# Cutting the last two query groups into units of two head slots by 128 queries, with one more joint maximum unit

## The chip, the cores and the metric

The kernel runs on one core of a Trainium2 chip. A core has TensorE (PE, matrix products), VectorE (DVE), ScalarE (ACT), GpSimd (POOL) and a queue engine (SP) that issues the transfers. Each works through its own list of instructions in order and waits for the others by semaphores. The metric is device microseconds of one execution, lower is better. The kernel before takes 1231.28 us, the median of 3 runs (1231.07 to 1231.67).

## The reference

One transformer block on 2048 tokens of width 512, batch 1, in bf16: LayerNorm, attention with 32 heads of 16 channels, output projection and residual, LayerNorm again, and a gated feed-forward layer of width 1792 with a second residual.

```python
    def _A_ref(x, wqkv, wo):
        ...
        qkv = (lambda x, *d: x.transpose(*d))((x @ wqkv).reshape(B, S, 3, H, Dh), 2, 0, 3, 1, 4)
        q, k, v = qkv[0], qkv[1], qkv[2]
        scores = jnp.einsum("bhqd,bhkd->bhqk", q, k) * (Dh ** -0.5)
        p = _softmax(scores, axis=-1)
        o = jnp.einsum("bhqk,bhkd->bhqd", p, v)
        return (lambda x, *d: x.transpose(*d))(o, 0, 2, 1, 3).reshape(B, S, D) @ wo

    def _B_ref(x, w_gate, w_up, w_down):
        return (_gelu(x @ w_gate) * (x @ w_up)) @ w_down

    x = A_x
    h = x + _A_ref(_layernorm(x, axis=-1), A_wqkv, A_wo)
    h2 = h + _B_ref(_layernorm(h, axis=-1), B_w_gate, B_w_up, B_w_down)
    return h2
```

## The kernel before

The 2048 tokens are cut into 8 groups (gi, 0 to 7) of 256 queries, and the 32 heads into 8 slots of 4 heads. A slot's 4 heads lie on the four row groups of 32 partitions, so four heads' products can stand side by side in PE's array. One unit (ui) is one group and one slot, 64 units in all, numbered group by group. A unit has 16 ticks, and the loop over ticks writes the instructions of all engines out in their order. That order is fixed when the program is built: a stream of dense work (projections, feed-forward) is fitted in by a planner (`Dense`, `PoolStream`) that keeps estimates of how far ACT and POOL have fallen behind.

Each unit is passed twice. The first pass (`p1_pair`, L841; `p1_consume`, L856) makes scores with the queries on the partitions, 512 keys at a time, and DVE reduces them to row maxima, one instruction over 1024 columns a tick. POOL turns the maxima into three bf16 pieces (`negm_pre`), a transposing transfer brings them to the key side, and POOL adds them to the spare rows of Q (L905), so that the second pass gets scores with the maximum already taken off. The second pass (`p2_tile`, L921; `p2_consume`, L950) runs 24 ticks later (16 + LAGX): scores with the keys on the partitions, 128 keys by 256 queries a matmul, two matmuls to a bank of 512 columns, and one Exp of 512 columns on ACT for each bank. Two such tiles belong to a tick. `item_pv` (L964) multiplies the exps with V, four heads side by side, in four steps a unit of 16 matmuls each. A 17th column of ones in V gives the sums. `o_turn` and `o_norm` (L998, L1002) transpose the result by a transfer and divide on POOL into `Otok`.

A unit in JOINT is a joint maximum unit. PE makes the differences of two key blocks for two heads, ACT takes their Relu into RB, and DVE adds and maximises in one pass (L853): two instructions over 512 columns take the place of two over 1024, and the unit loses one tick.

When a group's 8 slots are done, its 2 x 128 tokens get output projection and residual (`item_oproj`), LayerNorm on POOL, a transposing transfer into `hnT_l`, and then the feed-forward layer in the loop of the next groups: seven pairs `item_gate`, `item_up` (L1198, 256 columns), evacuated by ACT (L685), gelu by POOL's polynomial and a Tanh on ACT (L1178, L1186 to L1190), product on POOL (L1242), and two `item_down` (L1250). Where a tick has no dense work, filler matmuls keep PE going (`dummy`, L1410).

The end is different, since nothing is left to hide the last group behind. After tick 1024 no maxima are left; the 24 ticks of exps still due follow as exps of 1024 columns (`p2_pair`, L938), two to a block, with the dense items between the blocks. The flag `dve_free` then sends evacuations to DVE. The POOL and PE orders stay fixed: an instruction that waits holds everything behind it on its engine. Then `tail_b` does the rest for all 256 tokens of group 7: norm of the last slot (`tail_norm`), transposes, projection (L1361), bn_stats and scaling on DVE (L1364 to L1375) with a power on POOL (L1373), transposes (`tail_hnT`, L1335), and gate, up and down straight on PE, with Gelu on ACT (L1211) and the product on DVE (L1227).

## Time and profile before

| what | us |
|---|---|
| median of 3 runs | 1231.28 |
| the profiled execution | 1231.23 |
| its span, first to last instruction | 1229.3 |
| busy in the span: PE, DVE, ACT, POOL | 1104.8, 1175.8, 1189.5, 834.6 |
| end of the last maximum (DVE) | 1176.85 |
| end of the last exp (ACT) | 1200.10 |
| first gate matmul of the end | 1207.85 |
| end of the last copy before the store (ACT) | 1226.92 |

All places in the profile are counted from the start of the span; the execution's own time is 1.9 us longer than the span. The granted clock of TensorE is 1.0 throughout. Rows of groups read: line, engine, operation, tiles and shapes, count, then busy time, mean ns of one, and idle time of that engine ahead of them. Rows of stages read: stretch, length, then busy us and count of PE, PE's weight loads, DVE, ACT and POOL, granted clock, share of the DMA engines and GB/s. Rows of the order in time read: start, length of the merged row, engine, line, operation, tiles and shapes, count. A PE row's length includes the way through the array, so neighbours overlap; the pace is read from the starts. The chain's rows are start, length, engine, tile and line.

### The profile page before, as it was taken

Reading aid. Unit: us, or ns where it says so; the run is one execution under the profiler, and the core shown is the slowest. Engines: PE = TensorE matmul, PEld = TensorE weight load, DVE = VectorE, ACT = ScalarE, POOL = GpSimd, SP = SyncE. Lnnn points to the kernel's source line nnn. Section 1 sums busy time; section 2 is a strip of 40 time slices with the busy share of each in tenths; the row PEclk is TensorE's granted clock in tenths of the full one; section 3 lists DMA queues with packets and bytes.
Section 4 is the critical chain, followed back from the end, with each engine's and each line's share of the span. In section 5 each row is a group of like instructions: output and inputs, shape, how many; then the busy total and the mean of one; then the engine's idle time right before and its main releaser. Section 6 shows DMA issues by size and latency. Waiting matters only on the chain.

```text
span 1229.3 us, 31435 instructions
## 1 busy us (share of the span) xinstructions
PE 1104.8 (90%) x12462; PEld 429.5 (35%) x12598; DVE 1175.8 (96%) x1111; ACT 1189.5 (97%) x2417; POOL 834.6 (68%) x1760
## 2 busy tenths in 40 slices
PE   7899988889998989898989989999888988889898
PEld 3233232233333333333332333333333333333335
DVE  8999999999999999999999999999999999999933
ACT  7899999999999999999999999999999999999993
POOL 7567684766776586757768477775867777548850
PEclk9999999999999999999999999999999999999999
DMA  4111114200010000100011000100001100010000
GB/s 153 27 34 27 29 26 136 87 10 9 8 27 21 14 9 8 31 21 7 11 25 18 17 11 7 28 21 13 10 8 26 27 8 11 18 32 10 8 19 14
DMA packets 68658, 31.54 MB, mean 26 GB/s; under 512 B 53920, under 2 KB 67488, under 8 KB 68512
## 3 DMA queue, kind: packets, MB, share of 16 engines
q1 hardware_dynamic: 68512, 29.52, 9.5%
q8 instruction: 101, 1.65, 0.5%
q14 instruction: 45, 0.37, 0.1%
HBM read 11.80 MB, written 2.10 MB: 11 GB/s over the span
## 4 chain that ended last, share of the span: by engine, by line
ACT 57%; DVE 29%; PE 8%; issue 3%; POOL 2%; DMA 0%; POOLq 0%; DVEq 0%
ACT PTM L950 32%; DVE PM L856 29%; ACT PTG L950 10%; ACT PTE L950 6%; PE pbank L1250 2%; ACT g_sb L685 2%; ACT u_sb L685 2%; ACT th_sb L1178 2%; PE pbank L841 1%; PE pbank L921 1%; PE pbank L1198 1%; ACT OB L685 1%; PE pbank L443 1%; DVE OA L853 1%; PE pbank L1410 1%
## 5 line engine op out<-in xcount | busy, mean ns | idle before, releaser
L856 DVE TENSOR_REDUCE PM<-pbank 128x2 f32<-128x1024 f32 x998 | 1135.9, 1212 | 8.3 <-PE pbank L921 3.8
L950 ACT ACTIVATE PTM<-pbank 128x512 bf16<-128x512 f32 x1357 | 731.9, 719 | 3.9 <-PE pbank L921 0.4
L921 PE MATMUL pbank<-QT,KT 32*128 32x256 bf16 x4096 | 503.0, 273 | 14.8 <-ACT PTM L950 7.6
L841 PE MATMUL pbank<-KT,QT 32*128 32x512 bf16 x2022 | 388.6, 384 | 31.5 <-DVE PM L856 11.8
L1410 PE MATMUL pbank<-ones_bf,ident 128*128 128x512 bf16 x708 | 221.4, 384 | 52.2 <-ACT PTM L950 22.5
L950 ACT ACTIVATE PTG<-pbank 128x512 bf16<-128x512 f32 x407 | 224.8, 704 | 1.7 <-PE pbank L921 1.3
L841 PEld LDWEIGHTS pbank<-KT,QT 32*128 32x128 bf16 x2022 | 97.9, 90 | 363.4 <-DVE PM L856 139.0
L921 PEld LDWEIGHTS pbank<-QT,KT 32*128 32x128 bf16 x4096 | 170.3, 92 | 75.9 <-ACT PTM L950 40.4
L950 ACT ACTIVATE PTE<-pbank 128x512 bf16<-128x512 f32 x236 | 139.3, 717 | 1.3 <-PE pbank L921 0.9
L964 PE MATMUL pbank<-PTM,VA 128*17 128x256 bf16 x2776 | 125.4, 274 | 1.5
L998 POOL TENSOR_TENSOR LINV<-OBT,negone 128x8 f32<-128x8 bf16 x62 | 103.5, 1670 | 2.7 <-DMA OBT<-OB 2.7
L1188 POOL TENSOR_TENSOR th_sb<-g_sb 128x512 f32<-128x512 f32 x49 | 51.0, 1041 | 76.5 <-ACT g_sb L685 76.5
L1410 PEld LDWEIGHTS pbank<-ones_bf,ident 128*128 128x128 bf16 x810 | 47.8, 97 | 149.1 <-ACT PTM L950 94.9
L964 PEld LDWEIGHTS pbank<-PTM,VA 128*17 128x17 bf16 x2776 | 60.0, 89 | 45.5 <-issue 29.8
L1198 PE MATMUL pbank<-hnT_l,wg_sb 128*128 128x256 bf16 x448 | 67.0, 275 | 4.1 <-ACT PTM L950 0.9
L1198 PE MATMUL pbank<-hnT_l,wu_sb 128*128 128x256 bf16 x448 | 67.1, 275 | 2.1
L1187 POOL TENSOR_TENSOR th_sb<-th_sb,g_sb 128x512 f32<-128x512 f32 x49 | 62.3, 1270 | 4.1
L1190 POOL TENSOR_TENSOR th_sb<-th_sb,g_sb 128x512 f32<-128x512 f32 x49 | 62.1, 1268 | 1.7
L1242 POOL TENSOR_TENSOR GUT<-th_sb,u_sb 128x512 bf16<-128x512 f32 x49 | 62.1, 1268 | 1.2
L1250 PE MATMUL pbank<-wd_sb,GUT 128*128 128x512 bf16 x209 | 57.7, 382 | 2.8 <-ACT PTM L950 1.3
L905 POOL TENSOR_TENSOR QT<-QT,STG 128x256 bf16<-128x256 bf16 x64 | 42.8, 669 | 23.0 <-DMA STG<-ST 22.3
L1186 POOL TENSOR_SCALAR th_sb<-th_sb 128x512 f32<-128x512 f32 x49 | 30.4, 620 | 39.7 <-ACT th_sb L1178 39.7
(168 smaller groups left out, 1130.2 us busy)
## 6 DMA issues: line engine op xcount, KB each, us to landing
QKS<-QKS SPq DMA_DIRECT2D x27, 112.0 KB, 2.1
x_sb<-in_A_x_dram SPq DMA_DIRECT2D x4, 512.0 KB, 5.7
xres<-in_A_x_dram SPq DMA_DIRECT2D x16, 128.0 KB, 2.3
out_dram<-out_sb SPq DMA_DIRECT2D x16, 128.0 KB, 1.7
wg_sb<-in_B_w_gate_dram SPq DMA_DIRECT2D x4, 448.0 KB, 4.3
wu_sb<-in_B_w_up_dram SPq DMA_DIRECT2D x4, 448.0 KB, 3.9
wd_sb<-in_B_w_down_dram SPq DMA_DIRECT2D x3, 512.0 KB, 4.3
STG<-ST SPq DMA_TRANSPOSE x64, 2.3
```

Of the source, the lines that this page charges most:

```text
L841: P.op("pe", lambda e, g=g, b=b: e.matmul(pbank[:, b, :], QT[32 * g:32 * g + 32, c, slot, 128 * qt:128 * qt + 128], KT[32 * g:32 * g + 32, ...
L856: P.op("dve", lambda e: e.tensor_reduce(out=PM[:, par, qt, kc, g:g + 2], in_=pbank[:, b:b + 2, :], axis=AX.X, op=ALU.max), reads=[("pb", b ...
L921: P.op("pe", lambda e, kt=kt, i=i: e.matmul(pbank[:, b, 256 * i:256 * i + 256], KT[32 * g:32 * g + 32, slot, 128 * kt:128 * kt + 128], QT[ ...
L950: P.op("act", lambda e, b=b, pi=pi: e.activation(out=PTt(pi), in_=pbank[:, b, :], func=ACT.Exp), reads=[("pb", b)], writes=[("PT", pi)], e ...
L964: P.op("pe", lambda e, g=g, kt=kt, pi=pi, i=i: e.matmul(pbank[32 * g:32 * g + 17, b, 0:256], VA[:, kt, 4 * slot + g, :], PTt(pi)[:, 256 * ...
L998: P.op("pool", lambda e: e.tensor_tensor(out=li, in0=o4[:, :, :, 16], in1=negone[:, 0:8].rearrange("p (q h) -> p q h", q=2), op=ALU.pow), ...
L1187: o(1.27, lambda e: e.tensor_tensor(out=ts_, in0=ts_, in1=gs, op=ALU.mult), [("th", par), ("g", par)])], then=done)
L1190: o(1.27, lambda e: e.tensor_tensor(out=ts_, in0=ts_, in1=gs, op=ALU.mult), [("th", par), ("g", par)])], then=poly_done)
L1198: P.op("pe", lambda e, dc=dc, fc=fc, i=i: e.matmul(pbank[:, b, 256 * i:256 * i + 256], w[:, dc, 128 * fc:128 * fc + 128], hT[:, dc, :], st ...
L1242: P.op("pool", lambda e: e.tensor_tensor(out=o_ap, in0=shp(ts_), in1=shp(us), op=ALU.mult), reads=[("th", par), ("u", par)], writes=o_keys ...
L1250: P.op("pe", lambda e: e.matmul(pbank[:, b, :], GUT[:, fc, 128 * k:128 * k + 128], wd_sb[:, fc, :], start=first, stop=last), reads=[("GUT" ...
L1410: P.op("pe", lambda e: e.matmul(pbank[:, b, :], ident[:], ones_bf[:, 0:512], start=True, stop=True), reads=["ident", "ones_bf"], writes=[( ...
```

## The change

Groups 6 and 7 (GH = 6 and up) keep 8 units each, but a unit there is two slots by 128 queries: first the four slot pairs with the group's first 128 queries (half 0), then the same four with the second 128 (half 1). So a group's first 128 tokens have all heads after four units. A second-pass bank holds four matmuls of 128 columns, and a V step has 32 matmuls of 128 columns.

Group 6's feed-forward is done per half, in items of four chunks of 128 channels (`item_gate_h`, `item_up_h`, the last of two chunks). Group 7's first half goes through projection, LayerNorm and transposes behind tick 1024 (`item_oprojA`, `item_hnA`), with DVE and one POOL power, and its gate and up products are written out raw to GA and UA (`item_raw`) between the last exps; `tail_b` takes their gelu and product, and their down projection, beside the second half's norm. Only the second half then has gate, up and down at the very end (`tail_gate`, `tail_up`, `end_mm`), the down product as two halves of 256 columns with two stores. `item_down` may start behind tick 1024 without the planner's other conditions, and raw items are sorted ahead of it. The last unit's V steps come in two items. Unit 60, the first of group 7's second half, becomes the 14th joint unit. The diff, cut to its core:

```diff
+PV_TL = (9, 10, 17, 18)
+DOWN_AT = 2
+A_LATE = True
+GH = 6
-JOINT = (5, 9, 12, 14, 17, 20, 25, 28, 33, 36, 41, 44, 49)
+JOINT = (5, 9, 12, 14, 17, 20, 25, 28, 33, 36, 41, 44, 49, 60)
...
+        GA = at("GA", [128, NFC, 128], FP32, 0)
+        UA = at("UA", [128, NFC, 128], FP32, NSLOT * 512 * 2)
...
-        units = [(gi, slot) for gi in range(NG) for slot in range(NSLOT)]
+        UB = GH * NSLOT
+        units = [(gi, slot) for gi in range(GH) for slot in range(NSLOT)] + [(gi, 2 * sp) for gi in range(GH, NG) for _ in range(2) for sp in range(NSLOT // 2)]
+        half = lambda ui: (ui - UB) // (NSLOT // 2) % 2
+        def part(ui, qh):
+            gi, slot = units[ui]
+            hf = gi % 2
+            return (slot, 2 * hf + qh) if ui < UB else (slot + qh, 2 * hf + half(ui))
...
-            if it[0] is item_down and it[1] == (GL - 1, 1) and not force[0]:
+            if it[0] is item_down and not force[0] and not dve_free[0] and (tight() or dense.now // 16 in JOINT and dense.now % 16 > J_GONE - 6 or act_lag[0] > LAG_START):
                 return False
...
+            n, q0, kt0 = 2, 256 * hf, 2 * m
+            if ui >= UB:
+                slot, qt = part(ui, m // 4)
+                n, q0, kt0 = 4, 128 * qt, 4 * (m % 4)
+            qn = 512 // n
+            for i in range(n):
+                kt = kt0 + i
+                P.op("pe", lambda e, kt=kt, i=i: e.matmul(pbank[:, b, qn * i:qn * i + qn], KT[32 * g:32 * g + 32, slot, 128 * kt:128 * kt + 128],
+                                                          QT[32 * g:32 * g + 32, c, slot, q0:q0 + qn], start=True, stop=True, tile_position=(32 * g, 0)),
...
+        def add_ffn_half(gi, k):
+            for t in range(NTL):
+                dense.add(item_gate_h, gi, k, t, est=3)
+                dense.add(item_up_h, gi, k, t, est=3)
...
+        def item_oprojA(b):
...
+            P.op("dve", lambda e: e.bn_stats(out=stats2[:, t, :], in_=pbank[:, b, :]), reads=[("pb", b)], writes=[("stats2", t)])
+            P.op("dve", lambda e: e.tensor_copy(out=hh, in_=pbank[:, b, :]), reads=[("pb", b)], writes=[("h", GL % 2, 0)])
+            P.op("dve", lambda e: e.bn_aggr(out=mv2[:, t, :], in_=stats2[:, t, :]), reads=[("stats2", t)], writes=[("mv2", t)])
...
+            def rest():
+                P.op("dve", lambda e: e.tensor_scalar(out=hn_sb[:, 0, :], in0=hh, scalar1=mv2[:, t, 0:1], scalar2=rstd2[:, tt], op0=ALU.subtract, op1=ALU.mult),
...
+                dense.add(item_hnA, front=True, est=1, not_before=dense.now + 1)
+            pool.add([(0.6, lambda: P.op("pool", lambda e: e.tensor_tensor(out=rstd2[:, tt], in0=rstd2[:, tt], in1=nhalf[:, 0:1], op=ALU.pow), reads=[("rstd2", t), "nhalf"], writes=[("rstd2", t)]))], then=lambda: defer(1, rest), front=True)
...
+        def half_mms(b, gi, k, t, w, nm, hr):
+            fcs = chunks(t)
+            for i, fc in enumerate(fcs):
+                for dc in range(4):
+                    P.op("pe", lambda e, dc=dc, fc=fc, i=i: e.matmul(pbank[:, b, 128 * i:128 * i + 128], w[:, dc, 128 * fc:128 * fc + 128], hnT_l[gi % 2][:, dc, 128 * k:128 * k + 128], start=(dc == 0), stop=(dc == 3)),
...
+        def item_raw(b, t, w, nm, dst, key):
+            yield from half_mms(b, GL, 0, t, w, nm, [("hnT", GL % 2, 0)])
...
+            evac_act(dst[:, 4 * t:4 * t + n, :].rearrange("p c s -> p (c s)"), pbank[:, b, 0:128 * n], [("pb", b)], [(key, t)], extra=dQ)
...
+            for t in range(NTL):
+                raw_gelu(t)
+            raw_mult(0)
...
+            end_h()
+            gb = [4, 5, 6, 7, 3]
+            for t in range(NTL):
+                tail_gate(gb[2 * t % 5], t)
+                tail_up(gb[(2 * t + 1) % 5], t)
+                if t == 0:
+                    for fc in range(8, NFC):
+                        down_mm(0, GL, 0, fc)
...
+                if t >= 2:
+                    for q in range(2):
+                        end_mm(q, chunks(t - 2))
+            for q in range(2):
+                end_mm(q, range(4 * (NTL - 2), NFC))
```

478 lines of the change are left out of this document (297 added, 181 removed).

## The prediction

> **What bounds the kernel now.** I read the page first, then the list of groups for the stretch that the change touches, then busy time by stage, then the chain that ended last, and last the order of time on each engine behind the attention loop.
>
> ```profile
> span 1229.3 us, 31435 instructions
> PE 1104.8 (90%) x12462; PEld 429.5 (35%) x12598; DVE 1175.8 (96%) x1111; ACT 1189.5 (97%) x2417; POOL 834.6 (68%) x1760
> ```
> ```profile
> L856 DVE TENSOR_REDUCE PM<-pbank 128x2 f32<-128x1024 f32 x237 | 269.5, 1212 | 1.6 <-PE pbank L921 1.1
> L921 PE MATMUL pbank<-QT,KT 32*128 32x256 bf16 x952 | 117.6, 273 | 3.3 <-ACT PTM L950 1.9 <-ACT PTG L950 0.5
> L1410 PE MATMUL pbank<-ones_bf,ident 128*128 128x512 bf16 x150 | 47.2, 384 | 16.0 <-ACT PTM L950 9.0 <-ACT PTG L950 1.3 <-ACT OB L685 1.3
> ```
> ```profile
> 905.00:1176.85 271.85, 242.10 (x2860) 95.50 (x2888) 270.24 (x241) 269.62 (x557) 194.28 (x399) 1.00 0.07 17
> 1176.85:1200.12 23.27, 22.02 (x268) 9.39 (x272) 1.97 (x4) 22.98 (x29) 10.55 (x16) 1.00 0.07 21
> 1200.12:1207.85 7.73, 7.46 (x56) 3.50 (x49) 4.25 (x13) 3.65 (x6) 0.70 (x1) 1.00 0.00 0
> 1207.85:1229.30 21.45, 18.32 (x138) 13.60 (x140) 5.53 (x8) 4.78 (x8) 0.00 (x0) 1.00 0.06 20
> ```
> ```profile
> 1140.01 0.49 ACT u_sb L685
> ...
> 1154.08 22.76 DVE PM L856 x20
> ...
> 1223.69 2.60 PE pbank L1250 x12
> 1226.32 0.60 ACT out_sb L1403
> ```
>
> The shares of the page hide four stages with three different limits. In the attention loop (to 1176.85) DVE is the bound: 237 maxima stand idle 1.6 us together, and twenty of them take 22.76 us, 1.138 us each: one tick. ACT is nearly full beside it. From 1176.85 to 1200.12 the exps of the last 24 ticks drain on ACT (22.98 of 23.27 us busy; DVE 1.97). From there to 1207.85 runs a chain of small steps (last head's norm, output projection, LayerNorm), and from 1207.85 PE alone is the bound: gate, up and down of the last 256 tokens, 18.4 us of matmuls end to end, then one copy and the store.
>
> In the programs' order both kernels are alike until the add of unit 48's maximum (L905), near 905 us, so nothing can move ahead of that.
>
> **The change part by part.** Everything below is set against this profiled execution: span 1229.3, its own time 1231.23, which is 0.05 under the median of the three runs shown (1231.28).
>
> *Units of two slots by 128 queries (groups 6 and 7).* A score tile is four matmuls of 128 moving columns where it was two of 256; each step of probabilities times V is 32 where it was 16. Same columns, twice the weight loads. What a 128-column matmul costs with a weight load of its own:
>
> ```profile
> 10.15 1.06 PE L421 MATMUL pbank<-ident,xn_sb 128*128 128x128 bf16 x16
> ```
> ```profile
> L1335 PE MATMUL pbank<-ident,OnT 128*128 128x128 bf16 x8 | 0.7, 222 | 0.1
> ```
> ```profile
> 1167.53 0.39 PE L921 MATMUL pbank<-QT,KT 32*128 32x256 bf16 x2 [0.44 <-ACT PTM L950]
> 1168.40 0.39 PE L841 MATMUL pbank<-KT,QT 32*128 32x512 bf16 x2
> 1168.40 0.50 PE L921 MATMUL pbank<-QT,KT 32*128 32x256 bf16 x4
> 1168.83 0.40 PE L964 MATMUL pbank<-PTG,VA 128*17 128x256 bf16 x8
> 1169.05 0.39 PE L964 MATMUL pbank<-PTM,VA 128*17 128x256 bf16 x8
> 1169.38 0.39 PE L841 MATMUL pbank<-KT,QT 32*128 32x512 bf16 x2
> ```
>
> Sixteen transposes in 1.06 us, less the 0.22 that one takes, are 56 ns apart. Two score matmuls of one row group take 0.39 with 0.27 for the second: 120 ns apart for 256 columns. So a tile streams for 120+107 = 227 ns now and about 67+55+55+53 = 230 ns afterwards. V: 16 from 1168.83 to 1169.44 (four side by side, 109 ns a round) become 8 rounds of 56, 448 for 436 ns. A tick with a whole V step takes PE 0.98 us (1168.40 to 1169.38) against DVE's 1.138, and the 150 filler matmuls (L1410) of the stretch give way too. Cost 0; were the cover gone, 64 V steps by 12 ns plus 28 half FFN items by 24 ns would be 1.4 us. The FFN of group 6 is done in two halves of 128 tokens: the same columns again, the first half four units earlier, and ACT's evacuations and tanhs add up to the same in 512-column pieces. Group 6's first down projection moves from the end into the loop, where PE has room.
>
> *The 14th joint unit.* One maximum over 1024 columns falls out and another becomes two of 512:
>
> ```profile
> 915.04 0.68 DVE L853 CUSTOM_DVE_ANT_0 OA<-pbank,OA 128x512 f32<-128x512 f32 x1
> 915.65 0.69 DVE L853 CUSTOM_DVE_ANT_0 OA<-pbank,OA 128x512 f32<-128x512 f32 x1
> 916.26 9.29 DVE L856 TENSOR_REDUCE PM<-pbank 128x2 f32<-128x1024 f32 x8
> ```
>
> 915.04 to 916.26 is 1.22, in place of 2 x 1.138: DVE gains 1.06 us. ACT pays two Relus (0.49 each, as its other 512-column evacuations) and catches up two exps. If ACT can't, nothing is gained (bound 0). I take -0.8, near the full gain, because the moved FFN half leaves the last units of the loop less gelu work.
>
> *The drain.* It now holds the output projection and LayerNorm of the last group's first 128 tokens, and their gate and up (8 items, 112 matmuls by 56 ns), evacuated by the idle DVE.
>
> ```profile
> 1177.36 2.85 ACT L938 ACTIVATE PTG<-pbank 128x1024 bf16<-128x1024 f32 x3 [0.27 <-PE pbank L921]
> 1182.80 0.67 ACT L1178 ACTIVATE th_sb<-th_sb 128x512 f32<-128x512 f32 x1
> 1196.11 3.99 ACT L938 ACTIVATE PTM<-pbank 128x1024 bf16<-128x1024 f32 x4
> 1180.06 1.67 POOL L998 TENSOR_TENSOR LINV<-OBT,negone 128x8 f32<-128x8 bf16 x1
> 1205.40 0.70 POOL L1373 TENSOR_TENSOR rstd<-rstd,nhalf 128x2 f32<-128x2 f32 x1 [12.15 <-DVE rstd L1372]
> ```
>
> 24 exps of 1024 columns by 0.926 and one tanh (0.52 of path) make the 22.74 us from 1177.36 to 1200.10. The tanh is of 256 columns now (-0.2). PE is in order, and the transposes of the normalised half (item_hnA) stand behind the third block of scores. Counted from the last maximum: projection done 1.6; bn_stats 0.7, copy 0.65, aggregate and add 0.4: 3.35; the power and its two hops 0.88; scaling 0.4, transposes 0.4, copy 0.4: 5.5; first raw gate 0.9; then the fourth block of scores at 6.5, with its first exp at 6.9, where ACT is free at 6.06. **Stall 0.85.** On POOL the power (0.70) now stands ahead of a reciprocal (1.67) and the last unit's add, which ends at 6.5: the last unit is the fifth block, so that is in time. After that a block has 1.85 us and PE needs 1.7 to 2.0 (24 x 56 ns, or 64 V matmuls, scores 0.23, three changes of array form at some 0.11), so ACT stays the bound, narrowly. Sum +0.65; bounds -0.2 (no stall) and +3 (PE late by 0.3 in each of ten blocks).
>
> *From the last exp to the last gate input.* Before 7.75 us.
>
> ```profile
> 1195.56 0.69 DVE L674 CAST out_sb<-pbank 128x512 bf16<-128x512 f32 x1 [4.52 <-PE pbank L1255]
> 1200.60 0.42 DVE L674 COPY OA<-pbank 128x256 f32<-128x256 f32 x1 [4.35 <-PE pbank L964]
> 1203.61 0.70 DVE L1364 BATCH_NORM_STATS2 stats<-pbank 128x6 f32<-128x512 f32 x1 [0.57 <-PE pbank L1361]
> 1206.21 0.73 DVE L1375 TENSOR_SCALAR OnT<-xres,mv,rstd 128x512 bf16<-128x512 bf16 x2 [0.88 <-POOL rstd L1373]
> ```
>
> One token tile instead of two saves a bn_stats (0.6), half of each copy and one projection matmul (0.7 together). But eleven down matmuls and the residual (12 x 0.215 = 2.6) now stand on PE right ahead of the last V step, and the cast of 0.69 ahead of the OA copy on DVE: the V step ends some 0.9 later against the last exp. And four down matmuls and two residual ones (1.1) stand between the transposes and the first gate, of which 0.2 is covered. I get 7.5: -0.25, bounds -1.4 and +1. The four gelus of the raw half (0.6 each) and the table load lie beside this chain on ACT.
>
> *Gate, up and down at the end.*
>
> ```profile
> 1207.85 1.03 PE L1198 MATMUL pbank<-hnT_l,wg_sb 128*128 128x256 bf16 x8
> 1208.72 1.04 PE L1198 MATMUL pbank<-hnT_l,wu_sb 128*128 128x256 bf16 x8
> 1223.53 2.75 PE L1250 MATMUL pbank<-wd_sb,GUT 128*128 128x512 bf16 x12
> ```
> ```profile
> L1250 PE MATMUL pbank<-wd_sb,GUT 128*128 128x512 bf16 x53 | 13.1, 379 | 0.2
> L1410 PE MATMUL pbank<-ones_bf,ident 128*128 128x512 bf16 x31 | 8.4, 381 | 0.6 <-issue 0.3 <-DVE OA L674 0.3
> L1227 DVE TENSOR_TENSOR GUT<-pbank,th_sb 128x512 bf16<-128x512 f32 x7 | 4.8, 692 | 11.8 <-PE pbank L1198 11.8
> L1211 ACT ACTIVATE th_sb<-pbank 128x512 f32<-128x512 f32 x7 | 4.2, 597 | 11.6 <-PE pbank L1198 11.6
> ```
>
> Now: 112 matmuls of 256 at 109 ns (8 in 0.87) and 28 of 512 at 0.215 (12 in 2.75, of which the last takes 0.38), 18.44 us from 1207.85 to the last one's end. Afterwards: 112 of 128 at 56 ns = 6.27, six left-over down matmuls 1.29, 28 of 256 at 109 = 3.05, and 0.2 of latency: 10.8. ACT's gelu (0.6) and DVE's product (0.69) stay under PE's 0.9 an item. -7.64.
>
> By the Trainium skill, "TensorE: Matmul & The Clock Gate", section Back-to-back issue gap, a stream of load and matmul pairs sustains one per about 81 ns at 128 columns. By that the sum would be 112 x 25 ns = 2.8 us higher; the sixteen transposes at 56 ns speak against it here.
>
> *Store.* The last copy is 256 wide, 0.4 for 0.60 us; two half stores in place of one: -0.2.
>
> **Sum:** -0.8 + 0 + 0.65 - 0.25 - 7.64 - 0.2 = -8.24. 1231.23 - 8.24 = **1223.0 us**.
>
> **The rivals.**
>
> *PE becomes the bound in the last two groups (slower).* If a matmul can't start faster than its weight load allows, width no longer counts: at the 120 ns that the score matmuls show now, a tile would take 0.48 for 0.23 and a V step 0.87 for 0.44. Per tick, with a V step in one of four, +0.25+0.11 = 0.36 us, less PE's slack of 1.138-0.98 = 0.16: +0.2 in 240 ticks, 48 us, time about 1271. It decides from the point where the excess eats 8.24 us, 0.034 a tick: six extra spacings a tick, so (0.16+0.034)/6 = 32 ns each, 88 ns a matmul. For it: loads of one row group follow one another, and no row shows four 128-wide matmuls in one row group. Against it: the transposes, and L1198 with 109 ns a matmul, which is all stream.
> The Trainium skill has the rule behind it (same page, section The mechanism of packing small matmuls): a weight load overlaps running matmuls only where the row group differs. By that rule each load would stand open, as in this rival. The 109 ns of L1198, all rows of the array, don't agree with it.
>
> *The drain goes to PE.* Stalls of 0.3 us in every block, or the LayerNorm chain late by more than a block: +3 in place of +0.65, near 1225.5. For it: PE has 22.02 of 23.27 us busy there already. Against it: 31 matmuls behind 1177 are filler (L1410, 8.4 us), most of them in the drain.
>
> *The joint unit doesn't fit.* ACT, at 269.62 of 271.85, takes the two Relus on the path: +1 in place of -0.8, near 1224.8.
>
> *No change.* The end chain's new order costs what the halved FFN saves: it needs 7.6 us more between the last exp and the last gate, where every step is shown at 0.2 to 0.9. 1231.
>
> **How the numbers follow.** Forecast 0.61, drain on PE 0.16, joint unit 0.09, PE-bound groups 0.11, no change 0.03. A change of under 0.2% (2.5 us) can't be told from none. Faster: 0.61+0.16+0.09 = 0.86; same 0.03; slower 0.11. The lower end takes the favourable bounds (joint -1.06, drain -0.2, chain -1.4: 1220.8) and some room, 1219.5; the upper end takes the drain and the joint unit together (1227.2) with room, 1228.5. Left out: slower 0.11, same 0.03, and 0.04 at the ends.
>
> **What would show it.** The last maximum should end 0.5 to 1 us earlier; score matmuls of 128 should start some 56 to 67 ns apart in a row group, and DVE's idle time before maxima stay near 2 us behind 905. In the drain one idle gap of ACT near 0.9 us before the fourth block; from the last exp to the first tail gate about 7.5 us; from there to the last matmul 10.8. Wrong would be: maxima that wait for PE throughout groups 6 and 7, a drain over 26 us, or tail gates 80 ns or more apart.

## The result and the profile after

The changed kernel takes 1225.16 us (median of 4 runs, 1224.78 to 1225.74) beside 1231.43 (4 runs, 1231.07 to 1231.67) for the kernel before: a ratio of 0.995, 95% interval 0.9932 to 0.9967. The forecast was 1223.0 with a range of 1219.5 to 1228.5. The profiled execution, the longest of the four, took 1225.74 us, 5.5 less than that of before; 8.2 were forecast. By the median 2.2 us are missing against the forecast, in the profiles 2.7; what follows says where these 2.7 us are.

The page of the changed kernel first (span; busy time of each engine), then its busy time by stage (stretch, length, busy us and count of PE, PE's weight loads, DVE, ACT and POOL, granted clock, DMA share, GB/s), cut at the last maximum, the last exp and the first tail gate:

```profile
span 1224.0 us, 36091 instructions
PE 1130.3 (92%) x14845; PEld 476.7 (39%) x14845; DVE 1181.1 (96%) x1124; ACT 1190.3 (97%) x2421; POOL 841.3 (69%) x1774
```
```profile
905.00:1177.75 272.75, 255.29 (x4825) 140.94 (x4823) 270.35 (x243) 271.16 (x561) 194.75 (x403) 1.00 0.09 18
1177.75:1201.76 24.01, 22.54 (x535) 15.88 (x536) 9.27 (x21) 23.13 (x28) 14.08 (x23) 1.00 0.08 19
1201.76:1210.51 8.75, 6.27 (x94) 3.12 (x91) 4.82 (x11) 4.33 (x8) 4.17 (x4) 1.00 0.05 17
1210.51:1224.00 13.49, 10.77 (x148) 9.49 (x145) 2.92 (x5) 3.16 (x6) 0.00 (x0) 1.00 0.07 21
```

The stages stand one under the other, and against before's they read so:

| stage | before | after | forecast of the difference | measured |
|---|---|---|---|---|
| loop, to the last maximum | 1176.84 | 1177.75 | -0.8 | +0.91 |
| drain, to the last exp | 23.26 | 24.01 | +0.65 | +0.75 |
| last exp to first tail gate | 7.75 | 8.75 | -0.25 | +1.00 |
| gate, up, down to the last matmul | 18.43 | 10.77 | -7.64 | -7.66 |
| last copy and store | 3.00 | 2.69 | -0.2 | -0.31 |

The last column adds up to the spans' own difference, -5.31 us; another 0.18 of the 5.5 lies outside the spans. So the large term was right to 0.02 us, the drain to 0.1, and two small ones had the wrong sign: the loop is 1.7 us longer than forecast and the chain behind the last exp 1.25 us.

The widths first. These rows are the order in time on PE, in the loop and at the first tail gates:

```profile
1168.52 0.39 PE L943 MATMUL pbank<-QT,KT 32*128 32x128 bf16 x4
...
1210.51 1.06 PE L1292 MATMUL pbank<-hnT_l,wg_sb 128*128 128x128 bf16 x16
1211.40 1.06 PE L1292 MATMUL pbank<-hnT_l,wu_sb 128*128 128x128 bf16 x16
```

Four score matmuls of 128 columns in one row group take 0.39 us with 0.22 for the last, so they start 57 ns apart; sixteen gate matmuls take 0.89 from 1210.51 to 1211.40, 56 ns each. A load does not hold a narrow matmul up, in one row group or over the whole array. The rival with PE as the bound is gone, and so is the 81 ns of the Trainium skill ("TensorE: Matmul & The Clock Gate", section Back-to-back issue gap): no run here shows it.

The drain, on ACT (the bracket is ACT's idle time ahead of the row and what ended it):

```profile
1182.22 1.94 ACT L960 ACTIVATE PTM<-pbank 128x1024 bf16<-128x1024 f32 x2 [0.40 <-PE pbank L943]
1184.65 3.85 ACT L960 ACTIVATE PTM<-pbank 128x1024 bf16<-128x1024 f32 x4 [0.48 <-PE pbank L943]
```

The forecast had one stall of 0.85 us before the fourth block. There are two, 0.40 before the third and 0.48 before the fourth, 0.88 together, and nothing behind them: PE keeps up, if narrowly (22.54 of 24.01 us busy).

The chain behind the last exp, which ends at 1201.76. On PE, DVE and POOL in order of time:

```profile
1199.48 2.55 PE L1391 MATMUL pbank<-wd_sb,GUT 128*128 128x512 bf16 x11
1202.63 0.62 PE L989 MATMUL pbank<-PTM,VA 128*17 128x128 bf16 x32
...
1206.66 0.68 DVE L1490 TENSOR_TENSOR GUT<-GA,UA 128x512 bf16<-128x512 f32 x1
1206.82 0.93 POOL L1543 TENSOR_TENSOR rstd<-rstd,nhalf 128x1 f32<-128x1 f32 x1 [1.68 <-DVE rstd L1542]
1207.73 1.26 POOL L1490 TENSOR_TENSOR GUT<-GA,UA 128x512 bf16<-128x512 f32 x1
1207.87 1.27 DVE L1547 TENSOR_SCALAR OnT<-xres,mv,rstd 128x512 bf16<-128x512 bf16 x1 [0.52 <-POOL rstd L1543]
...
1209.19 0.40 PE L1469 MATMUL pbank<-ident,OnT 128*128 128x128 bf16 x4 [2.08 <-DVE OnT L1547]
```

The last V step ends at 1203.25, 1.49 us behind the last exp (some 0.5 before), held up by eleven down matmuls; the forecast had 0.9 of that delay. What was not: the scaling on DVE takes 1.27 us (the forecast took 0.4 from the same operation) while a POOL product of 1.26 us (1207.73) runs beside it, with a second one behind that; and the power takes 0.93 us where the row of before has 0.70, beside a DVE product. (Before had two columns there; the same power on one column took 0.58 us in the drain, L1207.) Against the rows of before that is 1.1 us on the chain.

In the loop, DVE's idle time before maxima is 2.4 us from 905 on (1.6 before), so within the forecast's "near 2", and still the last maximum is late:

```profile
L867 DVE TENSOR_REDUCE PM<-pbank 128x2 f32<-128x1024 f32 x235 | 268.5, 1214 | 2.4 <-PE pbank L943 1.3
```

### The profile page after: what moved, and what is told of

Same layout as the page of the kernel before. It is cut to its first block, busy times and chain, and to the rows that moved or that the text cites. A ratio compares the mean times of both kernels' runs of the same rounds, so it can differ in the third digit from the quotient of the medians.

```text
span 1224.0 us, 36091 instructions
## 1 busy us (share of the span) xinstructions
PE 1130.3 (92%) x14845; PEld 476.7 (39%) x14845; DVE 1181.1 (96%) x1124; ACT 1190.3 (97%) x2421; POOL 841.3 (69%) x1774
## 4 chain that ended last, share of the span: by engine, by line
ACT 56%; DVE 32%; PE 8%; issue 2%; DMA 1%; POOL 1%; POOLq 0%; DVEq 0%
ACT PTM L972 32%; DVE PM L867 31%; ACT PTG L972 10%; ACT PTE L972 5%; PE pbank L1391 2%; ACT th_sb L1262 2%; ACT g_sb L696 2%; ACT u_sb L696 2%; PE pbank L943 1%; PE pbank L852 1%; ACT PTM L960 1%; ACT OB L696 1%; PE pbank L1292 1%; PE pbank L1587 1%; DVE OA L864 1%
## 5 line engine op out<-in xcount | busy, mean ns | idle before, releaser
L867 DVE TENSOR_REDUCE PM<-pbank 128x2 f32<-128x1024 f32 x996 | 1134.9, 1213 | 9.3 <-PE pbank L943 4.4
L943 PE MATMUL pbank<-QT,KT 32*128 32x256 bf16 (+1 forms) x5120 | 506.2, 250 | 14.6 <-ACT PTM L972 8.1
L1587 PE MATMUL pbank<-ones_bf,ident 128*128 128x512 bf16 x774 | 237.0, 384 | 29.2 <-ACT PTM L972 4.7
L943 PEld LDWEIGHTS pbank<-QT,KT 32*128 32x128 bf16 x5120 | 205.9, 92 | 69.0 <-ACT PTM L972 40.1
L989 PE MATMUL pbank<-PTM,VA 128*17 128x256 bf16 (+1 forms) x3470 | 126.0, 252 | 1.6
L1272 POOL TENSOR_TENSOR th_sb<-g_sb 128x512 f32<-128x512 f32 (+1 forms) x50 | 51.2, 1024 | 63.6 <-ACT g_sb L696 63.6
L1271 POOL TENSOR_TENSOR th_sb<-th_sb,g_sb 128x512 f32<-128x512 f32 (+1 forms) x50 | 62.4, 1248 | 4.0
L1274 POOL TENSOR_TENSOR th_sb<-th_sb,g_sb 128x512 f32<-128x512 f32 (+1 forms) x50 | 62.3, 1246 | 1.7
L1270 POOL TENSOR_SCALAR th_sb<-th_sb 128x512 f32<-128x512 f32 (+1 forms) x50 | 30.5, 611 | 40.9 <-ACT th_sb L1262 40.7
L767 POOL TENSOR_SCALAR QT<-QKS,qmask 128x512 bf16<-128x512 bf16 x30 | 46.9, 1568 | 13.3 <-ACT QKS L696 11.9
L1347 PE MATMUL pbank<-hnT_l,wg_sb 128*128 128x256 bf16 x336 | 51.2, 275 | 3.3 <-ACT PTM L972 0.7
L1383 POOL TENSOR_TENSOR GUT<-th_sb,u_sb 128x512 bf16<-128x512 f32 x42 | 53.3, 1268 | 1.3
```

Source lines behind the costliest of these rows:

```text
L867: P.op("dve", lambda e: e.tensor_reduce(out=PM[:, par, qt, kc, g:g + 2], in_=pbank[:, b:b + 2, :], axis=AX.X, op=ALU.max), reads=[("pb", b ...
L943: P.op("pe", lambda e, kt=kt, i=i: e.matmul(pbank[:, b, qn * i:qn * i + qn], KT[32 * g:32 * g + 32, slot, 128 * kt:128 * kt + 128], QT[32 ...
L989: P.op("pe", lambda e, g=g, kt=kt, pi=pi, i=i, s_=s_, c0=c0, qn=qn: e.matmul(pbank[32 * g:32 * g + 17, b, c0:c0 + qn], VA[:, kt, 4 * s_ + ...
L1271: o(1.27, lambda e: e.tensor_tensor(out=ts_, in0=ts_, in1=gs, op=ALU.mult), [("th", par), ("g", par)])], then=done)
L1274: o(1.27, lambda e: e.tensor_tensor(out=ts_, in0=ts_, in1=gs, op=ALU.mult), [("th", par), ("g", par)])], then=poly_done)
L1383: P.op("pool", lambda e: e.tensor_tensor(out=o_ap, in0=shp(ts_), in1=shp(us), op=ALU.mult), reads=[("th", par), ("u", par)], writes=o_keys ...
```

## The experiments

Theories at the start. A: DVE's scaling is slow because POOL's products run beside it. B: the joint unit 60 gives back what it saves. C: the down matmuls ahead of the last V step hold the chain up. D: narrow matmuls cost something in the loop after all. Rivals stand in the expectations.

One caution on reading them. The 760th maximum comes ahead of anything that these kernels change in the shapes or the order of instructions, and it ended anywhere from 902.95 to 904.36 us in the profiled executions. Part of this is the clock. In the two profiles that reach the maximum last (904.22 and 904.36, experiments 12 and 10) TensorE's granted clock stands at 0.50 for some 3.4 us from about 23 us on, as in no other profile here. Experiment 10:

```profile
23.20:26.60 3.40, 3.40 (x12) 0.90 (x11) 2.98 (x4) 2.56 (x4) 3.30 (x5) 0.50 0.00 0
```

Half a microsecond between two medians of four runs is therefore nothing; the stages inside a profile are sharper, and the loop's length is counted from that maximum below.

### 1. Without joint unit 60

```diff
-JOINT = (5, 9, 12, 14, 17, 20, 25, 28, 33, 36, 41, 44, 49, 60)
+JOINT = (5, 9, 12, 14, 17, 20, 25, 28, 33, 36, 41, 44, 49)
```

> The changed kernel without the 14th joint unit (60). Seen in the changed kernel: its maxima fall 0.9 us behind the kernel before up to unit 59 and only 0.1 to 0.4 us remain behind unit 60, so theory A (the joint unit gains its DVE time, 2 x 1.138 - 1.22 = 1.06 us, and the loss has another source) expects the last maximum 0.7 to 1.1 us later than in the changed kernel (1177.77), near 1178.6, and the time near 1226.0. Theory B (ACT has no room for the Relus, the unit gains nothing and is the reason that the loop ended late) expects the last maximum at 1177.8 or earlier and a time of 1224.2 to 1225.2.

1224.66 us (1224.47 to 1224.79 and a profiled run of 1226.98), ratio 0.9944, 0.9929 to 0.9959. The last maximum ends at 1177.70: the joint unit gains nothing that shows. These are the numbers of theory B; whether ACT is the reason, this run does not tell (experiment 11 looks again). The profiled run is slow for another reason, seen on PE behind the last exp and in the stage 1210 to 1213 (granted clock 0.62):

```profile
1208.81 0.59 PE L1469 MATMUL pbank<-ident,OnT 128*128 128x128 bf16 x4 [2.08 <-DVE OnT L1547]
...
1211.33 1.51 PE L1292 MATMUL pbank<-hnT_l,wg_sb 128*128 128x128 bf16 x16
```
```profile
1210.00:1213.00 3.00, 3.00 (x27) 2.26 (x26) 0.00 (x0) 0.12 (x1) 0.00 (x0) 0.62 0.00 0
```

PE stands idle for 2.08 us ahead of the tail transposes, as in the changed kernel, and here the clock fell: the first gates took 1.35 us to the next row for 0.89. In two profiled runs of the changed kernel (the one above and experiment 9) the same idle time left the clock at 1.00; in experiment 8 it fell as here. By the Trainium skill ("TensorE: Matmul & The Clock Gate", section The HAM clock gate) the gate looks at PE's work in windows of 3.4 us that run by themselves. The length agrees with the 3.4 us at 0.50 in experiment 10. If so, the same pause could do both, by where it falls; no run here tests that, and the pause is shorter than such a window.

### 2. POOL's last two products behind the scaling

```diff
-            raw_mult(2)
-            raw_mult(3)
             P.op("dve", lambda e: e.tensor_scalar(out=hn_sb[:, 1, :], ...
+            raw_mult(2, more=[("OH", 1)])
+            raw_mult(3, more=[("OH", 1)])
```

> The changed kernel, but GpSimd's two last products of the raw half (1.27 and 0.73 us) start only behind VectorE's scaling of the second half's LayerNorm, where they ran beside it. That scaling took 1.27 us in the changed kernel and 0.41 us in the kernel before. Theory A (the two engines slow each other when both work on SBUF) expects the scaling at 0.41 us again, the first gate of the end 0.8 us nearer to the last exp (7.9 us for 8.75) and the time 0.8 us lower, near 1224.3. Theory B (the scaling is slow by its own, for where its operands lie or since half as many tiles go through it) expects 1.27 us again and no change.

1224.45 us (1224.22 to 1225.49), ratio 0.994, 0.9923 to 0.9957. DVE's scaling, POOL's products and PE's first gates:

```profile
1207.51 0.41 DVE L1545 TENSOR_SCALAR OnT<-xres,mv,rstd 128x512 bf16<-128x512 bf16 x1 [0.52 <-POOL rstd L1543]
1208.00 1.95 POOL L1490 TENSOR_TENSOR GUT<-GA,UA 128x512 bf16<-128x512 f32 x2 [0.60 <-DVE OnT L1545]
1209.29 1.06 PE L1292 MATMUL pbank<-hnT_l,wg_sb 128*128 128x128 bf16 x16
```

The scaling is back at 0.41 us, the gate comes 7.89 us behind the last exp (1201.40) instead of 8.75: 0.86, exactly the 1.27 less 0.41. Theory A is shown for this place: the products beside it made the scaling long. In the changed kernel the scaling starts 0.14 us into a product of 1.26 us and ends 0.15 us behind that product's end (1207.73 + 1.26 + 0.15 = 1209.14); in experiments 3 and 9 it is 0.15 too. The Trainium skill ("SBUF — State Buffer", section SBUF: two separate sides) has a rule for such pairs: DVE, in a mode that uses both its port pairs, and GpSimd share one pair of ports, which the first to start holds for its whole instruction. The trace agrees in part: the scaling ends only behind the product, but 0.15 us behind it and not the 0.41 that it takes alone, so it did not stand still through the whole product as the records have it. The power still takes 0.93 here, since DVE's product still lies beside it; that part was not tried.

### 3. Group 6's second down projection behind the last V step

```diff
+            if it[0] is item_down and not force[0] and dense.now >= 16 * NU + 16:
+                return False
-FILL_A = 2
+FILL_A = 8
```

> The changed kernel, but group 6's last down projection (14 matmuls and the residual) does not start between the last exps: it fills PE's waits in the chain of the second half's norm and LayerNorm instead. In the changed kernel eleven of its matmuls stand ahead of the last V step, which ends 1.3 us behind the last exp. Theory A (that order delays the chain) expects the V step to end 0.4 to 0.5 us behind the last exp, the first gate at 7.9 to 8.3 us for 8.75 (a part comes back, since six of the matmuls now stand right ahead of the gate), the time 0.5 to 0.9 us lower. Theory B (the chain waits for the last exp and GpSimd, not for PE) expects no change within 0.2 us.

1225.39 us (1225.38 to 1226.64), ratio 0.9948: the gate came 9.16 us behind the last exp (1200.98), later than in the changed kernel (8.75) and not earlier.

```profile
1204.42 2.98 PE L1393 MATMUL pbank<-wd_sb,GUT 128*128 128x512 bf16 x13 [0.26 <-POOL GUT L1492]
1206.21 1.28 DVE L1549 TENSOR_SCALAR OnT<-xres,mv,rstd 128x512 bf16<-128x512 bf16 x1 [0.52 <-POOL rstd L1545]
1207.78 1.46 PE L1393 MATMUL pbank<-wd_sb,GUT 128*128 128x512 bf16 x6
1210.14 1.07 PE L1294 MATMUL pbank<-hnT_l,wg_sb 128*128 128x128 bf16 x16 [0.47 <-ACT out_sb L698]
```

The first half of the theory holds: V ends 0.45 us behind the last exp, and the scaling starts 5.23 us behind it instead of 6.11. But the scaling still collides (1.28), and the moved matmuls came out on the other side: six and the residual behind the transposes, and then the gate waits 0.47 us for ACT's copy of their bank. The gain of 0.9 was spent on PE. Experiment 5 does it again with PE's order written out.

### 4. The kernel before with halved matmuls

```diff
-            for i in range(2):
-                kt = 2 * m + i
+            n, qn = (1, 256) if ui < 48 else (2, 128)
+            for i in range(2):
+                kt = 2 * m + i
+                for h in range(n):
...
+                        n, qn = (1, 256) if ui < 48 else (2, 128)
+                        for h in range(n):
                             for g in range(4):
```

> The kernel before with nothing changed but this: in units 48 to 63 each score matmul of the second pass and each matmul with V is written as two of 128 columns with a weight load each. It measures the price of the narrow matmuls alone. The forecast's own term (0, or at most 1.4 us were PE uncovered) expects the last maximum within 0.5 us of the kernel before (1176.85). Theory B, from the changed kernel, where maxima fell behind by 0.9 us over units 49 to 59: some 7 ns a tick from the narrow matmuls, the last maximum 0.9 to 1.8 us later, the time 1232.2 to 1233.2. The rival of the forecast (loads exposed at 120 ns a matmul) expects 48 us, 1279.

1235.44 us (1234.91 to 1236.21, 7 runs), ratio 1.0029, 1.0018 to 1.004, and the last maximum at 1180.39: 3.55 later. A price on each narrow matmul would show as a lag that grows evenly. Instead the maxima keep before's pace to 0.01 us a tick, except at two places, near 1040 and near 1083 us. The first, on POOL and DVE, then the transfers of 1034 to 1042, and below it POOL's same add in the kernel before:

```profile
1039.68 0.67 POOL L905 TENSOR_TENSOR QT<-QT,STG 128x256 bf16<-128x256 bf16 x1 [2.26 <-DMA STG<-ST]
1040.92 2.58 DVE L856 TENSOR_REDUCE PM<-pbank 128x2 f32<-128x1024 f32 x2 [1.53 <-PE pbank L923]
```
```profile
q8 instruction: 1, 0.02, 0.7%
...
STG<-ST SPq DMA_TRANSPOSE x1, 4.4
```
```profile
1037.49 0.67 POOL L905 TENSOR_TENSOR QT<-QT,STG 128x256 bf16<-128x256 bf16 x1 [0.15 <-DMA STG<-ST]
```

The transposing transfer of a unit's maxima was issued at 1035.18 (1035.10 before) and took 4.4 us to land, not 2.3. One packet of instructions (16 KB) started at 1037.6, while it was under way. The granted clock adds to the loss:

```profile
1041.00:1044.50 3.50, 3.50 (x116) 2.64 (x104) 3.08 (x3) 2.80 (x6) 3.34 (x4) 0.51 0.02 5
```

Of the 2.3 us by which the maxima fall back here, 1.6 come with the first late one and 0.7 in the three ticks behind it, in which the clock is at 0.51. Near 1083 us, at a clock of 1.00, it is a transfer of `Otok` (issued 1079.24, packet at 1080.56, 3.9 us to land) that PE waits for, and 1.3 us are lost.

In the whole trace of before, 21 of 154 transposing transfers have a packet of instructions that lies wholly between their issue and their landing: they take 2.3 to 4.1 us, median 3.25, 14 of them over 3; the other 133 have a median of 2.3, two of them over 3. In the changed kernel it is 32 of 156, with 2.3 to 4.5, median 3.4, 18 of them over 3, and a median of 2.3 for the other 124. All transfers over 3 us (16 and 20) had a packet start while they were under way, but so had 17 and 20 shorter ones, and a long transfer has more time to meet a packet; the counts alone do not tell cause from effect. The pages (the part on DMA queues; before, then after) have more such packets in the kernel with more instructions:

```profile
q8 instruction: 101, 1.65, 0.5%
```
```profile
q8 instruction: 118, 1.93, 0.7%
```

So theory D fell in its plain form, and a new one (E) took its place: narrower matmuls are more instructions, more instructions are more fetches, and a fetch that meets a transposing transfer the loop waits for delays it by up to 2 us. Experiment 7 tests it.

### 5. PE's order in the tail written out

```diff
-                dummy(next(...), want - (cost or 0))
+                if tick == 16 * NU + 23:
+                    own_down(6)
+                else:
+                    dummy(next(...), want - (cost or 0))
...
-            fill(2)
+            own_down(3)
...
+            own_down(NFC)
             down_h(0, GL, 0)
...
-            fill(FILL_A)
+            dummy(banks.free[0], 2)
```

Here own_down(n) writes the next n down matmuls of group 6's second half, and the residual behind the last; the item for them is dropped.

> The changed kernel with the two POOL products behind the scaling, as in the second experiment, and with PE's order in the tail written out: of the 14 down matmuls of group 6's second half 6 stand ahead of the last V step, in the place of fillers, 3 beside the copy of OnT, 5 and the residual beside the LayerNorm; 4 of group 7's stand ahead of the tail transposes and 4 behind; the copy of group 6's output goes to DVE behind the copy of hnT. Theory (the 11 down matmuls and the residual ahead of the last V step hold the chain up by 0.9 us, as the prediction had it): the last V step ends 0.5 us behind the last exp instead of 1.5, the scaling starts some 5.2 us behind the last exp instead of 6.1, the first tail gate comes 7.0 us behind it (7.9 in the second experiment, 8.75 in the changed kernel), time about 1223.5. Rival (the chain is set by DVE, POOL and ACT, PE's order is covered): the gate stays at 7.9 and the time at 1224.4.

1223.25 us (1223.19 to 1224.48, 5 runs), ratio 0.9931, 0.9917 to 0.9944. PE and DVE behind the last exp (1200.95):

```profile
1200.57 0.84 PE L991 MATMUL pbank<-PTM,VA 128*17 128x128 bf16 x32
1206.18 0.41 DVE L1574 TENSOR_SCALAR OnT<-xres,mv,rstd 128x512 bf16<-128x512 bf16 x1 [0.52 <-POOL rstd L1572]
1206.65 0.40 PE L1498 MATMUL pbank<-ident,OnT 128*128 128x128 bf16 x4
1207.96 1.06 PE L1294 MATMUL pbank<-hnT_l,wg_sb 128*128 128x128 bf16 x16
```

V ends at 1201.41, 0.46 behind the last exp; the scaling starts 5.23 behind it; the gate comes at 7.01, as expected, and PE has no pause left (the transposes wait for nothing). Theory C holds: the forecast's 0.9 us were real, and they could be taken out.

### 6. The transposes of the first half one block later

```diff
-                dense.add(item_hnA, front=True, est=1, not_before=dense.now + 1)
+                dense.add(item_hnA, front=True, est=1, not_before=dense.now + 3)
```

> As the one before, with the transposes of group 7's first half (item_hnA) one block of exps later, so that no scores stand behind them while the LayerNorm runs. Theory (the 0.4 and 0.5 us idle gaps of ACT in the drain come from that wait alone): both gaps fall below 0.15 us, the drain takes 23.2 us instead of 24.0, the time falls by 0.8 against the one before, to about 1222.7. Rival (PE is full in the drain, as in the second rival of the prediction): the same raw gate and up work in fewer blocks makes new gaps of ACT, 0.6 us or more together, the drain stays at 23.8 to 24.5 and the time at 1223.5.

1223.49 us (1223.13 to 1224.55), ratio 0.9931; the drain takes 24.02 us, with 24.01 in experiment 5. On ACT:

```profile
1181.72 5.61 ACT L962 ACTIVATE PTM<-pbank 128x1024 bf16<-128x1024 f32 x6 [0.40 <-PE pbank L945]
1187.78 0.42 ACT L1264 ACTIVATE th_sb<-th_sb 128x256 f32<-128x256 f32 x1 [0.45 <-POOL th_sb L1276]
```

The gap before the fourth block is gone (six exps in one row), and 0.45 us of a new wait stand before a tanh that ACT now reaches earlier than POOL has its input. The gap of 0.40 before the third block stays: it has another cause: in the changed kernel's trace the last up matmuls of group 6 wait 0.47 us on PE for DVE's copy of the projection (L1200), and the third block's scores stand behind them. The rival's figures came (drain 23.8 to 24.5, time 1223.5), but neither account was right: the gaps did not come from that wait alone, and what was late next was POOL, not PE.

### 7. Experiment 4 with the instruction count shifted

```diff
-                        n, qn = (1, 256) if ui < 48 else (2, 128)
+                        n, qn = (1, 256) if ui < 47 else (2, 128)
```

> The kernel before with the score and V matmuls of units 48 to 63 in halves of 128 columns, as in the fourth experiment, and with the V matmuls of unit 47 in halves too: 64 more matmuls and 64 more weight loads ahead of the stretch that lost 3.5 us there. Theory (the losses near 1040 and 1083 us are transposing transfers that an instruction fetch happened to hit; where a fetch falls hangs on the count of instructions before it): the waits of 1.5 us at 1040.9 and 1.7 us at 1084.2 go, others may come elsewhere with other transfers; the last maximum ends between 1176.8 and 1179.3. Rival (the halves cost where PE has little slack): the same waits at the same places, the last maximum at 1180.4.

1233.61 us (1232.91 to 1235.07, 10 runs), ratio 1.0013, 1.0004 to 1.0022; the last maximum at 1178.48. With 128 more PE instructions the waits at 1040.9 and 1084.2 are gone. A new one stands at 1057.8, again behind a transposing transfer that met a packet of instructions (issued 1052.68, packet at 1054.4, 3.7 us to land), here POOL, then DVE:

```profile
1056.48 0.67 POOL L905 TENSOR_TENSOR QT<-QT,STG 128x256 bf16<-128x256 bf16 x1 [1.56 <-DMA STG<-ST]
1057.79 1.23 DVE L856 TENSOR_REDUCE PM<-pbank 128x2 f32<-128x1024 f32 x1 [0.77 <-PE pbank L923]
```

Here too the clock falls behind the wait (0.51 from 1057.4 to 1060.9 us): of the 1.5 us lost, 0.6 come with the first late maximum and 0.9 in the ticks at that clock. More narrow matmuls, and a last maximum 1.9 us earlier than in experiment 4 (1.4 counted from the 760th): a price on the width can't do that. Theory E stands, as far as a coincidence of times and a shift can show it; that the fetch itself slows the transfer was not isolated.

### 8. Eight of group 6's first down matmuls left out

```diff
-                down_mm(b, gi, k, fc)
+                if (gi, k) != (GH, 0) or fc % 3 == 0 or fc == NFC - 1:
+                    down_mm(b, gi, k, fc)
```

> The changed kernel with 9 of the 14 down matmuls of group 6's first half left out (so those 128 tokens lack most of their feed-forward product): one a tick instead of three in the last five ticks of the loop. Theory (three down matmuls of 0.215 us a tick beside the scores make PE the bound in the last ticks, where the last half us of the loop is lost): DVE's gaps of 0.27 and 0.23 us before maxima at 1170 and 1176 us go, the last maximum ends about 0.5 us earlier, at 1177.2, and the time falls as much, to 1224.6. Rival (the loss there comes from what the joint unit leaves undone on ACT): the last maximum stays at 1177.7 within 0.15 and the time at 1225.1.

The edit keeps six of the 14 (0, 3, 6, 9, 12 and 13), so eight are left out, and not nine. 1226.61 us (1224.43 to 1227.56): the median is longer with less work. The gap at 1176 is gone, the one near 1170 stays (0.26), and the last maximum ends at 1176.75, but the stages behind it, in a profiled run of 1227.47, show why that helped nothing:

```profile
1174.00:1177.00 3.00, 2.70 (x18) 1.16 (x18) 2.75 (x3) 2.70 (x6) 0.62 (x2) 0.70 0.01 1
1177.00:1180.00 3.00, 2.67 (x42) 1.40 (x43) 0.52 (x1) 2.67 (x4) 1.35 (x7) 0.73 0.00 0
```

With PE thinned out and no filler in its place the granted clock fell to 0.7, the drain took 25.05 us for 24.01, and the chain fell to the lower clock once more (0.54 from 1210 to 1213). The one run of the four whose granted clock was 1.0 took 1224.43, near the theory's 1224.6. The question is taken up again in experiment 12, with fillers.

### 9 and 10. The changed kernel and experiment 5 once more, side by side

> The changed kernel itself, once more, on the same chip and beside the next three. Expected 1225.2 us within 0.4.

> The kernel of the fifth experiment once more, beside the changed one: 1223.25 us within 0.4, so 1.9 below the changed kernel (1.75 of it by the gate's place, 8.75 to 7.0 us behind the last exp).

1225.32 us (1224.98 to 1225.84) and 1224.13 (1223.31 to 1224.74): 1.2 apart, not 1.9. In its profiled execution the second one reached the 760th maximum 1.12 us later (904.36 for 903.24), in a stretch where the two programs are the same; counted from there it is 2.09 us shorter (318.23 for 320.32). The fall of the clock near 23 us, shown above, lies in that stretch. The one run of experiment 10 with a granted clock of 1.0 took 1223.31, as expected; the other three, at 0.999, took 1223.91 to 1224.74.

### 11. Experiment 5 without unit 60

```diff
-JOINT = (5, 9, 12, 14, 17, 20, 25, 28, 33, 36, 41, 44, 49, 60)
+JOINT = (5, 9, 12, 14, 17, 20, 25, 28, 33, 36, 41, 44, 49)
```

> The kernel of the fifth experiment without unit 60 among the joint units: the question of the first experiment once more, now with a tail in which PE does not stand idle. Forecast's view (the joint unit is worth 0.8 to 1.06 us): 1224.0 to 1224.3, the last maximum 0.8 to 1.06 us later than in the fifth experiment. Theory after the first experiment (what DVE saves in the unit is given back in the ticks that prepare it and in those behind it): 1223.25 within 0.4, the last maximum within 0.3 of the fifth's.

1222.80 us (1222.47 to 1223.43), ratio 0.9933, 0.9917 to 0.995: the shortest of all, beside 1224.13 with the unit in the same comparison (1223.31 in the run of that kernel at a clock of 1.0). Counted from the 760th maximum it is 0.64 us shorter than experiment 10 (317.59 for 318.23), and none of that is in the loop. DVE around the joint unit in experiment 5, and the same stretch without it:

```profile
1114.29 1.23 DVE L869 TENSOR_REDUCE PM<-pbank 128x2 f32<-128x1024 f32 x1 [0.21 <-PE pbank L945]
1115.43 0.68 DVE L866 CUSTOM_DVE_ANT_0 OA<-pbank,OA 128x512 f32<-128x512 f32 x1
...
1116.64 19.61 DVE L869 TENSOR_REDUCE PM<-pbank 128x2 f32<-128x1024 f32 x17
```
```profile
1105.70 30.63 DVE L869 TENSOR_REDUCE PM<-pbank 128x2 f32<-128x1024 f32 x27
```

The unit does what the forecast says: 1115.43 to 1116.64 is 1.21 us for two ticks of 1.13, a gain of 1.05. But a gap of 0.21 stands ahead of it and some 0.3 us more are lost in the ticks that prepare it; and behind it seventeen maxima take (19.61 - 1.23) / 16 = 1.149 us each where 27 without the unit take (30.63 - 1.23) / 26 = 1.131, another 0.3 and more. From the 760th maximum the loop takes 273.77 and 273.65 us with it and 273.76 without. What the unit does cost is a tick: with it, the last gate and up items of group 6 slip into the drain (1180.0 and 1181.0 in experiment 10, 1171.1 and 1172.3 without it), which takes 24.0 us instead of 23.66.

### 12. Experiment 8 again, with fillers, on the kernel of experiment 5

```diff
+                if (gi, k) != (GH, 0) or fc % 3 == 0:
+                    down_mm(b, gi, k, fc)
                 if fc % 3 == 2:
-                    yield 3
+                    yield 3 if (gi, k) != (GH, 0) else 1
```

> The kernel of the fifth experiment with 9 of the 14 down matmuls of group 6's first half left out (those 128 tokens lack most of their feed-forward product), and this time with a filler in each of those ticks, so that PE has one down matmul and one filler a tick where it had three down matmuls. Theory (three down matmuls a tick make PE the bound in the last five ticks): the last of the two gaps of DVE, 0.22 us before a maximum at 1176, goes, the last maximum ends some 0.45 us earlier than in the fifth experiment (1176.5), TensorE's clock stays at 1.0 and the drain at 24.0, time 1222.8. Rival (the loss in the last ticks is ACT's debt from the joint unit): the last maximum within 0.15 of the fifth's and 1223.25 us.

1223.36 us (1223.09 to 1224.07), ratio 0.9938. DVE in the last ticks with three down matmuls a tick (experiment 10) and with one and a filler:

```profile
1170.69 5.87 DVE L869 TENSOR_REDUCE PM<-pbank 128x2 f32<-128x1024 f32 x5 [0.27 <-PE pbank L945]
1176.79 1.23 DVE L869 TENSOR_REDUCE PM<-pbank 128x2 f32<-128x1024 f32 x1 [0.22 <-PE pbank L945]
```
```profile
1170.88 6.95 DVE L869 TENSOR_REDUCE PM<-pbank 128x2 f32<-128x1024 f32 x6 [0.26 <-PE pbank L945]
```

From the first of these starts to the end of the last maximum it is 7.33 us against 6.95: 0.38 by the down matmuls, as the theory has it (0.45), with nine of them left out this time. The 0.26 ahead of 1170.88 stay; two V steps in neighbouring ticks stand there on PE. Over the whole loop the gain drowns in what other ticks lose: 273.61 us for 273.65, and the expected 1222.8 did not come.

### The stages side by side

Loop from the end of the 760th maximum to the end of the last one; the other columns as above, in us.

| kernel | loop | drain | exp to gate | gate to last matmul | end | median |
|---|---|---|---|---|---|---|
| before | 273.26 | 23.26 | 7.75 | 18.43 | 3.00 | 1231.43 |
| after | 274.20 | 24.01 | 8.75 | 10.77 | 2.69 | 1225.16 |
| 9, after again | 274.08 | 24.05 | 8.75 | 10.77 | 2.68 | 1225.32 |
| 2, products behind | 273.82 | 24.28 | 7.89 | 10.77 | 2.68 | 1224.45 |
| 5, tail order | 273.77 | 24.01 | 7.01 | 10.77 | 2.68 | 1223.25 |
| 10, the same again | 273.65 | 24.12 | 7.01 | 10.77 | 2.68 | 1224.13 |
| 11, without unit 60 | 273.76 | 23.66 | 7.01 | 10.77 | 2.39 | 1222.80 |

The changed kernel and experiments 2, 3, 5, 6, 9 and 10 issue the same instructions in the loop, and their loops take 273.65 to 274.20 us: differences of under half a microsecond in that column say little, and of before there is one profile only. The end is 0.3 us shorter without unit 60 (experiments 1 and 11); why was not followed up.

## Why the prediction was right, and where it was off

*What decides it.* Right, and by its own working: the tail's matmuls stream at their width (56 ns for 128 columns), half the tokens leave the end, and 18.43 us become 10.77 (forecast 10.8). This term alone makes the kernel faster; all the others together are 2.35 us on the other side.

*Units of two slots by 128 queries.* "Cost 0" held for the matmuls themselves: their pace is 57 ns where the forecast said 55 to 67, and experiment 4 shows none of its loss spread over the ticks. It left out one thing, the 4656 more instructions of the program and their fetches; in the kernel before, the halves alone cost 2.3 to 3.7 us of loop (experiments 7 and 4, 275.53 and 276.91 for 273.26), nearly all of it (experiment 4) or 1.5 us of it (experiment 7) in waits for transfers that met a packet and in the fall of the clock behind them. In the changed kernel's units no such loss shows: without unit 60 (experiment 11) the 986th maximum ends 259.53 us behind the 760th, 259.62 before. That is luck, as far as the runs show, since 32 of its 156 transposing transfers met a packet. The 0.5 us by which that loop is longer than before all come in the last twelve maxima. The step "group 6's first down projection moves into the loop, where PE has room" also failed, and it falls in that stretch: three down matmuls a tick, in the last five ticks, cost 0.38 us (experiment 12). PE has room on average and not there.

*The 14th joint unit.* This step failed: -0.8 forecast, nothing measured (experiments 1 and 11). The price of the unit on DVE was right (1.05 saved for 1.06). The reason for taking nearly all of it, less gelu work on the last units, was no row, only an argument; the 0.5 us ahead of the unit and the 0.3 and more behind it are what it left out. The rival "the joint unit doesn't fit" gave 1224.8 and was the nearest to what came, with the loss spread over some thirty ticks instead of lying on the Relus. So of the 1.7 us that the loop missed, some 0.8 are the joint unit's and some 0.5 come in the last twelve maxima; the remaining 0.4 is within the spread of loops with the same instructions.

*The drain.* Right in size (+0.75 for +0.65) and in its stall (0.88 for 0.85), in part by luck: the wait that was forecast, before the fourth block, came with 0.48, and the other 0.40, before the third, has a cause that the forecast did not have (experiment 6). The rival with PE as the bound of the drain did not come true; experiment 6 shows what is late next, and it is POOL.

*From the last exp to the last gate input.* The sign was wrong, +1.0 for -0.25. The 0.9 us by which the V step ends later were in the sum and came (experiment 5 takes them out). The sum has a slip on paper: with 0.2 of the 1.1 us ahead of the gate covered, as it is written, its terms add up to +0.5; -0.25 comes out only with 0.2 uncovered. The runs show about the latter: 1.32 us from the transposes to the gate, 1.17 before. What failed is the term that took each DVE and POOL step at its duration of before: with products now running beside them, the scaling took 1.27 us for 0.41 (its cause shown in experiment 2) and the power 0.93 for 0.70 (its cause not tried). The bound of +1 held, just.

*Store.* -0.31 for -0.2.

The range held because its upper end had been set by the drain and the joint unit going wrong together. They did not; the joint unit and the chain did.

## What to carry to other kernels

A step moved beside another engine's work does not keep its duration: when POOL gets a product to do "beside" a DVE step of the critical chain, look at what both read and write, and put the product behind the step if nothing needs it sooner; here that was 0.86 us for two lines. Room on an engine is read tick by tick, where the work will stand, and a saving in a stage with two full engines (a joint unit here) is worth what the ticks around it leave of it. When an edit multiplies the instructions, list the transfers that the loop waits for with little slack, since fetches may meet some of them; and a wait that leaves PE idle can be paid twice, by the clock behind it (experiments 4 and 7).

## What the runs showed of the hardware

- A DVE step of 0.41 us that starts 0.14 us behind the start of a 1.26 us POOL product ended 1.27 us after its own start (changed kernel); with the products behind it, 0.41 (experiment 2).
- Transposing transfers took 2.3 us at the median, and 3.3 to 3.4 with a packet of instructions wholly between issue and landing, up to 4.5 (kernels before and after). Shifting the program by 128 instructions moved the loop's waits and took 1.8 us off a kernel's median, 1.4 off its loop (experiments 4 and 7).
- A pause of 2.08 us of PE left the clock at 1.00 in two profiled runs of the changed kernel and lowered it in two others, to 0.62 and 0.54 over the next 3 us (experiments 1 and 8). With eight down matmuls taken out and no fillers it stood at 0.70 to 0.73 and the median was 1.3 us longer than the changed kernel's in experiment 9 (experiment 8).
- The clock stood at 0.50 to 0.51 for some 3.4 us behind a wait in the loop (experiments 4 and 7), and near 23 us in two profiles that then reached the same place some 0.4 us or more later than all others (experiments 10 and 12).
